# One weight load cut into other row groups: 96 + 8 + three strided groups of 8 rows in place of 112 + 5 + 5 + 5 + 1

## The chip, the cores and the metric

The kernel runs on one core of one Trainium2 chip. The metric is device time in microseconds (us) of the whole program on that core, the median of several runs. A profiled execution gives, beside its own time, a span (first to last instruction on the core) and a trace of instructions, semaphore events and DMA packets. Sixteen DMA engines move all data between HBM (the chip's main memory) and SBUF (the core's working memory).

## The reference, cut to what matters

Two stages follow each other. Attention over 4 batches, 8 heads, 768 positions and 64 head dimensions comes first; its output, reshaped to 3072 x 512, feeds a soft mixture of 8 experts. The weights of the experts are `w1` (8 x 512 x 1024) and `w2` (8 x 1024 x 512), in float32: 16 matrices of 2 MB each, 33.5 MB in all.

```python
logits = x @ phi
d = softmax(logits, axis=0);  slot_input = d.T @ x          # 32 slots, 4 of each expert
for e in range(E):
    slot_out[e] = maximum(slot_input[e] @ w1[e], 0) @ w2[e]
c = softmax(logits, axis=1);  out = c @ slot_out            # 3072 x 512
```

All the weights are read whole, however few the rows that go through them (4 slots for each expert).

## The kernel before, in words

One function builds the whole program. It describes the work as operations with dependences, costs and keys (`pl.op`), and a planner (`Plan.run`, L87) puts them into one order ahead of time; the order in which each engine gets its instructions follows from that. The planner's costs decide nothing at run time beyond the order.

**Loads.** q, k, v and the weights are loaded by the helper `dma` (L281). It makes three planner operations: the issue (a `gpsimd.dma_start`, so the instruction stands in POOL's queue, L283), the generation of the descriptors, and the landing (`dma_us`, L290, a cost by bytes and descriptors). The transfer converts float32 to bfloat16 on its way. There are 37 such transfers in one fixed order (the list `names`, L901, in which `w5` stands for five). All run on one software queue, called q0 in the profile, and each is spread over the DMA engines, which take their shares of the queue in the same order. An issue is planned behind the landing of the transfer eight places ahead of it (L907).

**A weight matrix as rows.** A `w1` matrix is seen as 128 rows (`(di do) f -> di do f`, `do=4`): row `di` is 16 KB of contiguous float32 in HBM and goes to SBUF partition `di`, where it takes 8 KB as bfloat16. A matrix loaded in one transfer of 128 rows (L364) gives each of 16 engines 8 rows.

**The uneven weight.** Matrix number `UNEVEN = 5` (`w5`, the sixth of `w1`) is the exception: the block at L355 to L363 loads it in five transfers into the one slot, and `landed w5` gathers them. The order of the queue around it is w3, w4, the five parts of w5, the rest of q and all of k and v of the last batch (`q3.64`, `k3.0`, `v3.0`), then w6 to w15. The last matrix, w15, comes in two halves of its columns (`w15a`, `w15b`, L350), 128 x 8 pieces each.

**The end of the program.** When attention is done, the matmuls of `w1` (L945) and then those of `w2`, expert by expert (`W2.0` to `W2.8`, emitted at L990), wait for the weights as they land. `W2.7` uses w15a and `W2.8` uses w15b. After each of the two, ACT scales the result (L1004), and PE, ACT and DVE form the output tiles (L1056, L1064, L1066). SP stores them on the hardware queue q1 (L1083): first six stores of 256 KB and one of 512 KB, then four of 1 MB.

Other traffic uses the same 16 engines: small tables and a first piece of w0 through q1 at the start, and fetches of instructions (queues q8 and q14), which the program does not issue itself.

Of the kernel before, what the change touches and what calls it, by code (L numbers as in the profile page):

```python
# [173 lines left out]
def kernel(  # L174
# [106 lines left out]
    def dma(name, key, nbytes, ndesc, buf, dst, src, deps=()):  # L281
        iss = pl.op("issue " + name, {"POOL": 0.62}, key, deps=deps, acq=[buf] if buf else [], lead=1.3,
                    emit=lambda o: nc.gpsimd.dma_start(dst(), src))  # L283
        issues.append(iss)
        gen = pl.op("gen " + name, {"GEN": 2.5 if name[0] == "w" and int(name[1:3].rstrip("abc")) > 5 else 1.45}, key, deps=[iss])
        land = pl.op("land " + name, {"DMA": dma_us(nbytes, ndesc) + LATE.get(name, 0.0)}, key, deps=[gen], lead=3.3)
        ring.setdefault(name, []).append((iss, land))
        return land

    def dma_us(nbytes, ndesc):  # L290
        return ndesc / 16 * 0.004 + nbytes / 16 / RATE
# [40 lines left out]
    def w_view(i):  # L332
        m = late_mem[i]() if i in late_mem else slots[wbuf[i].slot][:, :]
        return m.rearrange("p (a f) -> p a f", a=4 if i < NE else 8)

    def load_w(i, key, deps=()):
        if i == 0:

            flat = lambda: w_view(0).rearrange("p a f -> p (a f)")
            wland[0] = dma("w0", key, 7 << 18, 128, wbuf[0], lambda: flat()[:, WF:],  # L340
                           moe_w1[0].rearrange("(di do) f -> di (do f)", do=4)[:, WF:])
            w_cast.append(pl.op("CW", {"ACT": 0.6}, -90, deps=[wf_land], need=[wbuf[0]],
                                emit=lambda o: nc.scalar.copy(flat()[:, 0:WF], wf)))
            return
        if i < NE:
            src = moe_w1[i].rearrange("(di do) f -> di do f", do=4)
        else:
            src = moe_w2[i - NE].rearrange("(fi fo) d -> fi fo d", fo=8)
            if i == NW - 1:
                for k, (c0, c1) in enumerate(((0, CH), (CH, 512))):  # L350
                    last_lands.append(dma(f"w15{'ab'[k]}", key + 0.1 * k, (c1 - c0) << 12, 1024, None,
                                          lambda c0=c0, c1=c1: w_view(i)[:, :, c0:c1], src[:, :, c0:c1], deps=deps))
                wland[i] = last_lands[0]
                return
        if i == UNEVEN:  # L355

            buf, prev, land = wbuf[i], [], []
            for p0, p1 in ((0, 112), (112, 117), (117, 122), (122, 127), (127, 128)):
                land.append(dma(f"w{i}", key, (p1 - p0) << 14, p1 - p0, None if prev else buf,
                                lambda p0=p0, p1=p1: w_view(i)[p0:p1], src[p0:p1], deps=prev))  # L360
                prev = [issues[-1]]
            wland[i] = pl.op(f"landed w{i}", {"SP": 0.01}, key, deps=land)
            return  # L363
        wland[i] = dma(f"w{i}", key, 2 << 20, 128, None if i in late_mem else wbuf[i],  # L364
                       lambda: w_view(i), src, deps=deps)
# [151 lines left out]


    load_w(0, -30)
    for x in "ABC":  # L520
        load_tile(x, -29)
    load_w(1, -28)
    load_w(2, -27)
    for x in "DE":
        load_tile(x, -26)
# [103 lines left out]
    def evs(x, b, n):  # L629
        if b == 0:  # L630
            return ev[x, b]
        return [e for r0, r1, e in ev[x, b] if r0 < 24 * (n + 1) and r1 > 24 * n]
# [33 lines left out]
    for b in range(B):  # L666
        for n in range(4):
# [30 lines left out]
            for kk, g in enumerate(GORDER):  # L698
                sc = Buf("SC")
                key = k0 + kk * T / 5.3  # L700
# [17 lines left out]
                if g in (1, 3, 4):  # L718
                    m = {1: 0, 3: 1, 4: 2}[g]
                    masko[p, m] = pl.op(f"MK.{p}.{m}", {"DVE": [0.70, 0.70, 0.57][m]}, key + 0.3,  # L720
                                        deps=[expo[p, x] for x in ((0, 1), (2, 3), (3, 4))[m]] + o_hm[n],
                                        emit=mask_emit(b, n, m))

        for ns in ([(0, 1), (2, 3)] if b == 0 else [(0, 1, 2, 3)]):
            sc = Buf("SC")

            def emit_lx(o, b=b, sc=sc, ns=ns):
                sc_mms(sc, b, [(128 * x, n, XJ, XI, 1) for x, n in enumerate(ns)])

            key = T * (4 * b + ns[0]) + 0.9 * T  # L730
            a = pl.op(f"QX.{b}.{ns[0]}", {"PE": 0.09 * len(ns)}, key - 2.0, n=2 * len(ns),
                      deps=list(dict.fromkeys(e for n in ns for x in "qk" for e in evs(x, b, n))),
# [15 lines left out]
    for b in range(B):  # L748
        for n in range(4):
# [5 lines left out]
            for i in iorder:  # L755
                deps, need = [v2e[p], vfo[p]], set()
# [6 lines left out]
                def emit_pv(o, b=b, n=n, p=p, i=i):  # L763
                    pT = pTs[PTb[b, n].slot]
                    vb = vbs[VBb[b].slot]
                    for h in range(2):
                        for j in range(i + 1):
# [3 lines left out]
                            else:  # L771
# [5 lines left out]
                             deps=list(dict.fromkeys(deps)) + ([last] if last else []),  # L777
# [269 lines left out]
    for m, (gi, r, d0, d1) in enumerate(parts):  # L1047
# [7 lines left out]
        def emit_om(o, gi=gi, r=r, d0=d0, d1=d1, bank=bank, early=early):  # L1055
# [3 lines left out]
                  deps=[so_a if early else so_b], acq=[bf], emit=emit_om)  # L1059
# [8 lines left out]
        w = (d1 - d0) / 512  # L1068
# [39 lines left out]
    for o in order:  # L1108
# [9 lines left out]
        if front:  # L1118
# [3 lines left out]
            n = int(0.75 * (gap - 0.1) / unit + 0.5) if gap > 0.2 else 0  # L1122
# [23 lines left out]
        us, w = gap - (1.5 if o.name[:2] == "W2" else 0.12), 512 - c0  # L1146
# [53 lines left out]
```

## Time and profile before

| what | value |
|---|---|
| runs shown | 148.67, 148.75, 149.09 us; median 148.75 |
| profiled execution | 148.61 us, of which the span 146.8 (1.8 lie around it) |
| granted TensorE clock over the span | 0.965 |
| busy share of PE, DVE, ACT, POOL | 85%, 76%, 75%, 16% |
| q0 (software queue): packets, MB written | 6912, 26.09 |
| HBM read, written | 52.49 MB, 6.29 MB |
| w15b lands (last load) | 128.78 us into the span |
| last store of 1 MB lands | 145.9 us |

Times are in us from the start of the span, unless ns is written. A busy share is an average over stages that have different limits, so the views used below are the 40 slices of the span, the chain of work that ended last, the timeline around the last loads, and the DMA packets.

The trace holds two things of the DMA that are used below. For every transfer it has the 16 increments of its semaphore, one by each engine as its share has landed. For every packet it has the queue, the start, the duration and the size written, but not the engine. An engine runs its packets one behind the other, so that the packets can be joined into 16 chains by their starts; a chain is one engine, without its number.

### The profile page before, as it was taken

What the parts mean: (1) busy time and instruction counts of PE and PEld (TensorE: products, weight loads), DVE (VectorE), ACT (ScalarE), POOL (GpSimd) and SP (SyncE); (2) the same over time, 40 slices, a digit from 0 to 9 for tenths busy, and PEclk for the clock granted to TensorE, in tenths of its full rate; (3) what the DMA queues carried; (4) which work ended last, traced back from release to release, by engine and by line L of the source; (5) the groups of instructions that cost most, each with busy time, mean ns of one, the idle gap of its engine ahead of it and who ended that gap; (6) DMA issues with size and microseconds to landing.
All of it is one profiled execution on the core that took longest, in us unless ns stands there. A gap on an engine that the chain in (4) does not pass through costs nothing.

```text
span 146.8 us, 4972 instructions
## 1 busy us (share of the span) xinstructions
PE 125.4 (85%) x2171; PEld 80.9 (55%) x2171; DVE 111.6 (76%) x244; ACT 110.3 (75%) x143; POOL 24.0 (16%) x48
## 2 busy tenths in 40 slices
PE   6999899989899998999999999998778996679200
PEld 2365566668576675877576776765534564233000
DVE  3898399987999899899999999999847610249500
ACT  3374999989999999999998999999814700469600
POOL 6921110412011211110400211010700000100000
PEclk9999999999999999999999999999999999968955
DMA  4999999999999999999999999999999999979996
GB/s 100 190 214 215 225 204 211 218 210 228 214 206 212 215 223 214 219 214 203 211 216 224 212 214 219 216 216 214 214 219 214 216 215 186 137 246 392 413 415 250
DMA packets 9608, 33.03 MB, mean 225 GB/s; under 512 B 867, under 2 KB 4595, under 8 KB 7283
## 3 DMA queue, kind: packets, MB, share of 16 engines
q0 software_dynamic: 6912, 26.09, 88.8%
q1 hardware_dynamic: 2672, 6.62, 11.8%
q8 instruction: 17, 0.28, 0.7%
q14 instruction: 5, 0.04, 0.1%
q10 hardware_dynamic: 2, 0.00, 0.0%
HBM read 52.49 MB, written 6.29 MB: 400 GB/s over the span
## 4 chain that ended last, share of the span: by engine, by line
DMA 33%; PE 23%; DVE 15%; ACT 14%; POOL 4%; issue 4%; ACTq 0%; POOLq 0%
DMA slot<-in_v_dram 17%; DMA qk<-in_moe_w_dram 16%; ACT pt L713 9%; PE pv L773 7%; PE sc L641 6%; DVE pt L658 4%; DVE xv L787 3%; POOL slot L283 3%; PE tr L611 3%; DVE qk L278 2%; ACT slot L1064 2%; PE tr L799 2%; DVE xT L278 2%; PE tr L676 2%; PE sc L1056 1%
## 5 line engine op out<-in xcount | busy, mean ns | idle before, releaser
L713 ACT ACTIVATE pt<-sc 128x1024 bf16<-128x1024 f32 x80 | 76.8, 1045 | 3.0 <-PE sc L641 2.5
L641 PE MATMUL sc<-qk 64*128 64x512 bf16 (+3 forms) x256 | 31.2, 308 | 2.7 <-ACT pt L713 1.8
L658 DVE TENSOR_TENSOR pt<-pt,msk 128x1024 bf16<-128x1024 bf16 (+1 forms) x48 | 30.0, 640 | 0.5 <-ACT pt L713 0.4
L773 PEld LDWEIGHTS <-pt 128*128 128x128 bf16 x640 | 23.4, 97 | 6.7 <-issue 5.6
L773 PE MATMUL pv<-vx,pt 128*128 128x65 bf16 x352 | 26.1, 193 | 0.1
L773 PE MATMUL pv<-vf,pt 128*128 128x65 bf16 x288 | 20.9, 194 | 0.0
L641 PEld LDWEIGHTS <-qk 64*128 64x128 bf16 x256 | 10.3, 93 | 11.5 <-issue 4.5
L611 PE MATMUL tr<-ident,slot 128*64 128x128 bf16 (+1 forms) x448 | 15.5, 219 | 0.5 <-DMA slot<-in_v_dram 0.5
L787 DVE TENSOR_TENSOR xv<-pv,rs 128x768 bf16<-128x768 f32 x16 | 15.3, 957 | 0.6
L611 PEld LDWEIGHTS <-slot 128*64 128x64 bf16 (+1 forms) x448 | 12.7, 110 | 3.6 <-issue 3.2
L283 POOL DMA_DIRECT2D slot<-in_moe_w_dram x15 | 8.1, 541 | 39.8 <-PE tr L611 9.1
L278 DVE COPY qk<-tr 128x768 bf16<-128x768 bf16 (+2 forms) x24 | 12.9, 551 | 0.7 <-PE tr L611 0.4
L278 DVE COPY xv<-tr 128x768 bf16<-128x768 bf16 (+2 forms) x20 | 8.4, 432 | 2.9 <-PE tr L569 2.9
L799 PE MATMUL tr<-ident,xv 128*128 128x128 bf16 x96 | 8.1, 220 | 2.2 <-DVE xv L787 1.9
L278 DVE COPY xT<-tr 128x768 bf16<-128x768 bf16 x14 | 7.8, 554 | 1.0 <-PE tr L799 0.8
L1004 ACT ACTIVATE msk<-pv,rcs 128x256 bf16<-128x256 f32 x2 | 0.9, 474 | 10.0 <-PE pv L990 10.0
L799 PEld LDWEIGHTS <-xv 128*128 128x128 bf16 x96 | 5.7, 97 | 4.7 <-DVE xv L787 2.2
L1066 DVE TENSOR_SCALAR slot<-tr,rrow 128x256 f32<-128x256 f32 (+1 forms) x6 | 3.3, 571 | 6.5 <-PE tr L1056 6.4
L676 PE MATMUL tr<-ident,xv 128*128 128x128 bf16 x96 | 7.9, 220 | 0.1
L278 DVE COPY vx<-tr 128x768 bf16<-128x768 bf16 x14 | 7.7, 550 | 0.2 <-PE tr L676 0.2
L1157 PE MATMUL pv<-zero 128*128 128x512 bf16 x30 | 7.5, 382 | 0.0
L692 DVE TENSOR_TENSOR vf<-vx,fm 128x528 bf16<-128x528 bf16 x16 | 6.9, 430 | 0.3
(122 smaller groups left out, 172.3 us busy)
## 6 DMA issues: line engine op xcount, KB each, us to landing
slot<-in_moe_w_dram POOLq DMA_DIRECT2D x9, 1024.0 KB, 22.8
out_dram<-slot SPq DMA_DIRECT2D x4, 1024.0 KB, 5.9
slot<-in_q_dram POOLq DMA_DIRECT2D x3, 768.0 KB, 20.0
slot<-in_k_dram POOLq DMA_DIRECT2D x3, 768.0 KB, 15.1
slot<-in_moe_w_dram POOLq DMA_DIRECT2D x2, 896.0 KB, 23.1
slot<-in_v_dram POOLq DMA_DIRECT2D x2, 768.0 KB, 13.2
out_dram<-slot SPq DMA_DIRECT2D x6, 256.0 KB, 2.5
slot<-in_v_dram POOLq DMA_DIRECT2D x2, 512.0 KB, 24.2
```

The source lines that it names most:

```text
L278: nc.vector.tensor_copy(dst, src)
L283: emit=lambda o: nc.gpsimd.dma_start(dst(), src))
L611: nc.tensor.transpose(t[64 * i:64 * (i + 1), :, s, :], rv[:, i, 8 * c + s, :], ident[0:nr, 0:nr])
L641: nc.tensor.matmul(scb[sc.slot][:, i, c:c + 128 * nb], kk, qq.rearrange("p b c -> p (b c)"), start=True, stop=True)
L658: nc.vector.tensor_tensor(pw, pw, mw, op=ALU.mult)
L676: nc.tensor.transpose(t[:, 128 * j:128 * (j + 1)], vT[:, 6 * n + j, :], ident)
L692: nc.vector.tensor_tensor(vfs[VFb[p].slot], vv, fm[:, n], op=ALU.mult)
L713: nc.scalar.activation(pTs[PTb[b, n].slot][:, :, 512 * g:512 * (g + 1)], scb[sc.slot], ACT.Exp, scale=scale)
L773: nc.tensor.matmul(pvb[:, h, 65 * i:65 * (i + 1)], lt, rhs, start=(j == 0), stop=(j == i))
L787: nc.vector.tensor_tensor(xo, pvw[:, :, :, 0:64], r.rearrange("p i (j o) -> p i j o", o=1).to_broadcast([P, 2, 6, 64]), op=ALU.mult)
L799: nc.tensor.transpose(t[:, 128 * i:128 * (i + 1)], xv[:, i, 128 * n:128 * (n + 1)], ident)
L1157: nc.tensor.matmul(bank[:, c0:c0 + w], zero[:, 0:128], zero[:, 0:w], start=(c0 == 0), stop=True, skip_group_check=True)
```

## The change

The five transfers of `w5` take other rows. All five still go into the same slot, in the same place of the same queue, and every row is still loaded once. A third number, the step, is added to the row ranges, so that the last three transfers take every third row from 104 on: rows 104, 107, ... 125, then 105, ... 126, then 106, ... 127.

```diff
         if i == UNEVEN:
 
             buf, prev, land = wbuf[i], [], []
-            for p0, p1 in ((0, 112), (112, 117), (117, 122), (122, 127), (127, 128)):
-                land.append(dma(f"w{i}", key, (p1 - p0) << 14, p1 - p0, None if prev else buf,
-                                lambda p0=p0, p1=p1: w_view(i)[p0:p1], src[p0:p1], deps=prev))
+            for p0, p1, st in ((0, 96, 1), (96, 104, 1), (104, 128, 3), (105, 128, 3), (106, 128, 3)):
+                n = len(range(p0, p1, st))
+                land.append(dma(f"w{i}", key, n << 14, n, None if prev else buf,
+                                lambda p0=p0, p1=p1, st=st: w_view(i)[p0:p1:st], src[p0:p1:st], deps=prev))
                 prev = [issues[-1]]
             wland[i] = pl.op(f"landed w{i}", {"SP": 0.01}, key, deps=land)
             return
```

The row counts were 112, 5, 5, 5, 1 and become 96, 8, 8, 8, 8. The change's own title says that three rows more go to eight DMA engines, where they went to five.

## The prediction

> **What bounds the kernel now.** I read the 40 slices first, then the chain of work that ended last, then the timeline around the last loads, then the DMA packets.
>
> ```profile
> DMA  4999999999999999999999999999999999979996
> GB/s 100 190 214 215 225 204 211 218 210 228 214 206 212 215 223 214 219 214 203 211 216 224 212 214 219 216 216 214 214 219 214 216 215 186 137 246 392 413 415 250
> ```
>
> The DMA engines are full from the second slice to the 34th, at one rate. The dip in slices 34 and 35 (121 to 128.4 us) is the end of the loads; after it come the stores.
>
> ```profile
> 103.77 0.53 POOL pt L283
> 104.30 0.28 POOL qk L283
> 104.58 0.60 issue
> 105.17 23.61 DMA qk<-in_moe_w_dram
> 128.78 0.04 issue
> 128.82 0.43 PE pv L990 x8
> 129.25 0.02 issue
> 129.27 0.48 ACT msk L1004
> 129.75 0.04 issue
> 129.79 0.32 PE sc L1056
> ```
>
> In the chain, w15b is issued at 104.6 and lands 23.6 us later: it stands in a full queue. From 128.78 on everything hangs on it. The timeline shows that PE was ready:
>
> ```profile
> 128.08 0.27 PE L1056 MATMUL tr<-msk,expT 128*128 128x256 bf16 x1
> ...
> 128.28 0.09 PEld L990 LDWEIGHTS <-xT 128*32 128x32 bf16 x1 [0.22 <-issue]
> 128.82 0.40 PE L990 MATMUL pv<-qk,xT 128*32 128x256 bf16 x8 [0.47 <-DMA qk<-in_moe_w_dram]
> ```
>
> PE had the stationary matrix in at 128.28 + 0.09 and waited 0.47 us for the DMA. So the kernel is bound by the engine whose share of w15b lands last; from there to the end of the span it is 146.8 - 128.78 = 18.0 us. What was done ahead of it hangs on w15a, which the same engine brings last.
>
> **Sixteen engines, not one queue.** The 16 increments of three transfers, sorted, in us (from the trace's semaphore events):
>
> ```
> w4    63.51 63.61 63.66 63.85 63.89 64.00 64.01 64.38 | 64.72 64.73 64.77 64.80 64.83 64.91 64.92 65.12
> w6    81.42 81.48 81.80 | 82.53 82.61 82.62 82.72 82.94 83.13 83.49 83.55 83.66 83.67 83.85 83.99 84.53
> w15b  125.67 125.72 126.05 | 127.67 127.73 127.77 127.87 127.90 127.92 127.97 127.98 128.09 128.09 128.30 128.36 128.78
> ```
>
> Ahead of w5 eight engines lead by about 1 us; at the end three lead by about 2 us, and thirteen lie within 1.2. The packets say why. A row of a weight (8 KB written) comes every 606 ns on each engine. Queue q8 fetches 16 KB of instructions 16 times up to 117 us; such a packet takes 0.89 to 0.98 us and holds its engine up. Followed as chains, each of the eight late engines gets one of the eight fetches after w4; together with their lag at w4 that makes two each (an inference for the earlier ones). The three that lead keep exactly the same distances from 76 us to the end: no fetch at all. I call the eight late ones F (fetch) and the others N.
>
> Now w5 itself. After its 112-row transfer five chains, all in N, each show a row, an increment, a row, an increment, a row, an increment: the three transfers of 5 rows went to the same five engines, one row each. They take 6.20 us from the end of w4 to the end of w5, the rest of N 4.36: 1.84 us for three rows, about what two fetches cost. The single row 127 was cut into 16 pieces of 512 bytes, 41 ns each beyond their overlap. So the five are level with F at the end, and three engines of N have 2 us to spare.
>
> The last engine of all (128.78) is one of the five. At 80.04 a fetch of 8 KB on q14 falls into its chain, and its next row takes 838 ns instead of 625: 0.53 us in all. The last of F lands at 128.36.
>
> **The change part by part.**
>
> *Even part, 6 rows in place of 7.* 96 rows over 16 engines are 6 each. Each engine loses a row: -606 ns.
>
> *Rows 96 to 103.* The title's three rows more, for eight engines, fit only if these eight rows are shared evenly, half a row each (6.5 against 9.5). The trace has no such transfer. Its neighbours are the contiguous single row, cut into 16 pieces, and the contiguous 5 rows, not cut. Half a row is a packet of 4 KB, which other loads show: 304 ns from start to start. Bounds: half a row on each engine; a whole row on N and nothing on F; nothing on N and a whole row on F. I take the half row, since 8 rows, unlike 5, make 16 equal pieces of at most a row, as the title needs.
>
> *The strided rows.* Three transfers of 8 rows in place of three of 5. By the nearest row, 5 rows on the same five engines three times, I put them one each on the same eight engines, the five and the three others of N. A row costs 604 ns and its increment 21, as before: 1.88 us for three. An engine without a row passes such a transfer in 11 ns. A step in HBM and SBUF leaves the row at 16 KB read, 8 KB written; nothing shows another price. If a strided row cost more, the five have 0.34 us before they are later than now.
>
> *The row that falls away.* Row 127 alone: -41 ns, with its increment kept by the fifth transfer.
>
> The sums from the end of w4 to the end of w5, from these rows:
>
> - F: 4.26 + 0.03 + 0.06 = 4.36 before; 6 rows 3.655 + half row 0.325 + empty transfers 0.034 = 4.01 after: **-0.34**.
> - The five: 6.20 before; 3.655 + 0.325 + 1.878 = 5.86 after: **-0.34**.
> - The other three: 4.36 before, 5.86 after: **+1.50**. They land at 126.05 + 1.50 = 127.55 at the latest.
>
> The largest landing goes from 128.78 to 128.44, still by the same engine, while F ends at 128.02. The bytes are the same: thirteen engines give up 0.34 each (4.4 us together), which three that had idled take over (3 x 1.50).
>
> *What doesn't move.* POOL issues five transfers for w5 as before, 0.50 to 0.58 us each, and the queue holds over 20 us of work (w15b: 24 us from issue to landing), so a slower issue is hidden; it would cost only if the queue ran dry. In the planner the bytes up to the fifth part are equal, so q3.64 and all that follows keep their planned landings; only the planned issues of w6 to w9 can move, and they stand in POOL's queue, which between 72 and 103 us holds little else. From 31 to 104 us the chain is compute, so an earlier landing there brings nothing; the three delayed engines are still not the last for k3.0 and v3.0. What is late next: the same transfer, then PE, whose first half also moves by 0.34 since w15a ends 2.65 us before w15b on every engine. The stores start from the results, so I move the 18.0 us behind as a block.
>
> So the profiled time of 148.61 becomes 148.27, and the median, 0.14 above it, 148.75 - 0.34 = **148.41 us**, -0.23%. About 0.3% (0.45 us) is what a measurement of this kernel can tell from no change.
>
> **The rivals.**
>
> 1. *The first eight rows go whole to N too.* Then N gets 10 rows, F 6. The five: 3.655 + 4 x 0.626 = 6.16, -0.04; F -0.66; the three +1.80 (127.85). End 128.74: 148.71, no change. For it: the 5-row transfers were not cut. Against: the title's count of three. The Trainium skill, "DMA: Bandwidth & Descriptors", section "Why a DMA increments its semaphore by 16 and not by 1", has an exception for the software queue in which each engine gets the partitions divided by 16, rounded up, from engine 0 on; the trace's five engines agree, and eight rows would then go this way.
>
> 2. *The stride doesn't hold rows together, or the eight alternate.* All 16 engines then get 8 rows: F 3.655 + 4 x 0.325 = 4.96, +0.60, or with whole rows in turn +0.57. The five gain 1.2, but F now ends at 128.36 + 0.6 = 128.96: 148.93, slower by 0.12%. The decision is at F +0.42. Half a way (first eight rows cut, the three others in turn) gives F +0.28: 128.64, 148.6. For it: the trace has no strided rows. Against: three transfers in a row hit the same five. The same section of the skill states that fewer than 16 engines are taken from a round-robin cursor, which speaks for this rival; the trace's chains of three rows speak against it here.
>
> 3. *Three of the eight engines are fetch engines*, ending clearly slower. The trace gives no numbers to engines; that the three next to the five are the three idle ones I infer from the five all lying in N. An F engine with 9.5 rows gets +1.50: 127.67 to 128.36 become 129.17 to 129.86. It decides as soon as one lands behind 128.78, as every F engine would. Of three the last at about 129.6: +0.85, 149.6 us.
>
> 4. *First eight rows whole on F, the rest on N* (7 against 9): F -0.04, the five -0.66, end 128.32: 148.29. This is the largest gain that F allows.
>
> **How the numbers follow.** Forecast 60%; rival 1 14%; rival 2 11%; rival 3 9%; rival 4 3%; 3% for a step that I don't see (a reordered queue, another granted clock in the last stage, 0.72 now). Forecast with run spread (148.67 to 149.09 for one kernel) 148.2 to 148.65. The range, 148.15 to 149.0, takes in rivals 1, 2 and 4 and leaves out rival 3. Faster by over 0.3% means below 148.30: a quarter of the forecast's cases, half of rival 4's and a little of the rest: 0.22. Slower, above 149.20: rival 3, a little of rival 2 and of the unseen: 0.14. Within: 0.64.
>
> **What would show it right or wrong.** After: eight chains with three whole rows behind the increment of the first part, 16 packets of 4 KB in place of the 16 of 512 bytes, no engine that leads by 2 us in w15b, and its last landing near 128.44. Three leaders still there, or a new last one above 129, mean rival 3; 32 whole rows behind the first part mean rival 1; a spread of F to the back by half a microsecond, rival 2. It is wrong in its last step if w15b lands earlier and the end doesn't follow.

## The result, and the profile after

The changed kernel takes 149.79 us (median of 5 runs, 149.56 to 150.19) beside 148.74 for the kernel before (5 runs, 148.55 to 149.09): ratio 1.0074, 95% interval 1.0050 to 1.0099. That is slower by 1.05 us, where 0.34 less was forecast, and outside the range.

The 40 slices of the page of the changed kernel (profiled execution 149.56 us, span 147.8):

```profile
DMA  4999999999999999999999999999999999779995
GB/s 97 193 213 218 218 209 211 212 214 220 217 212 217 211 223 217 220 215 199 208 216 224 215 217 211 217 213 215 215 217 217 220 204 186 102 240 382 410 426 248
```

Up to the 34th slice the DMA digits are those of the kernel before. The 35th, at the end of the loads, has fallen from 9 to 7 tenths (137 to 102 GB/s); the 36th was at 7 already. The views by stage put numbers to it. Each line has the stretch, its length, the busy time of PE, PEld, DVE, ACT and POOL, and at its end the granted clock, the DMA share and GB/s. The kernel before:

```profile
125.60:128.80 3.20, 1.52 (x15) 0.88 (x15) 1.26 (x3) 1.78 (x4) 0.40 (x1) 1.00 0.81 114
128.80:146.80 18.00, 7.43 (x32) 2.91 (x31) 6.89 (x12) 7.91 (x14) 0.00 (x0) 0.72 0.90 350
```

The changed kernel:

```profile
126.70:129.90 3.20, 1.52 (x19) 0.89 (x18) 1.27 (x3) 1.78 (x4) 0.40 (x1) 1.00 0.44 63
129.90:147.80 17.90, 7.38 (x32) 2.81 (x31) 6.91 (x12) 7.90 (x14) 0.00 (x0) 0.73 0.90 352
```

In the last 3.2 us of the loads the DMA engines are 44% busy, where they were 81%: many have finished, and the loads wait for a few. The stage behind, 17.9 us, is as long as it was, within 0.1 us. The chain that ended last:

```profile
103.67 0.53 POOL pt L283
104.20 0.28 POOL qk L283
104.48 0.60 issue
105.07 24.77 DMA qk<-in_moe_w_dram
129.85 0.04 issue
129.89 0.43 PE pv L991 x8
```

w15b is issued 0.1 us earlier than before and lands at 129.85, 1.07 later. PE stood ready again, as the timeline has it:

```profile
129.36 0.09 PEld L991 LDWEIGHTS <-xT 128*32 128x32 bf16 x1 [0.22 <-issue]
129.89 0.40 PE L991 MATMUL pv<-qk,xT 128*32 128x256 bf16 x8 [0.46 <-DMA qk<-in_moe_w_dram]
```

The wait for the DMA is 0.46 us, where it was 0.47: what comes ahead of it has moved along with w15a. So the loss is that one landing: it moved by 1.07 us, and the span is 1.0 us longer. Its 16 increments, before and after:

```
before  125.67 125.72 126.05 | 127.67 127.73 127.77 127.87 127.90 127.92 127.97 127.98 128.09 128.09 128.30 128.36 128.78
after   125.08 125.35 | 127.33 127.43 127.46 127.46 127.57 127.70 127.70 127.71 128.00 128.08 128.23 128.64 | 129.68 129.85
```

Two engines still lead by 2 us, and two others are now a microsecond behind the rest. The DMA issues name the five parts of w5:

```profile
slot<-in_moe_w_dram POOLq DMA_DIRECT2D x1, 768.0 KB, 29.5
slot<-in_moe_w_dram POOLq DMA_DIRECT2D x4, 64.0 KB, 21.2
```

Four parts of 64 KB written, 8 whole rows each. The packets show how they were shared. There is no packet of 4 KB more than before, and of 512 bytes exactly 16 fewer (2048 on q0): rows 96 to 103 were not halved. The chains from the end of w4 on (left: end of w4 in ns; R a packet of 8 KB, | an increment, ' the 9 ns records of a transfer that brings nothing to this engine, h a 4 KB packet of q3.64):

```
N  63225 RRRRRR|R|R|R|R|hhhh|
N  63538 RRRRRR|R|R|R|R|hhhh|
N  63769 RRRRRR|R|R|R|R|hhhh|
F  64376 RRRRRR|R|R|R|R|hhhh|
F  64392 RRRRRR|'''''''hhhh|
```

Eight chains have four rows behind the sixth, the other eight none: 10 rows against 6. And the eight are not N: six of N and two of F (64376 and 64562). The two have the latest landings. By the terms of the prediction an engine with 10 rows takes 3.655 + 4 x 0.626 = 6.16 us for w5, where F took 4.36: +1.80, and the latest of F, 128.36, would be 130.16 at most, the earliest 129.47. The two are at 129.68 and 129.85.

### The profile page after: what moved, and what is told of

Read it like the earlier page. It is cut to its first block, busy times and chain, and to the rows that moved or that the text cites. A ratio compares the mean times of both kernels' runs of the same rounds, so it can differ in the third digit from the quotient of the medians.

```text
span 147.8 us, 4972 instructions
## 1 busy us (share of the span) xinstructions
PE 124.7 (84%) x2171; PEld 80.6 (55%) x2171; DVE 111.8 (76%) x244; ACT 110.2 (75%) x143; POOL 23.9 (16%) x48
## 4 chain that ended last, share of the span: by engine, by line
PE 28%; DMA 24%; ACT 20%; DVE 16%; issue 4%; POOL 1%; ACTq 1%; POOLq 0%
DMA qk<-in_moe_w_dram 17%; ACT pt L714 14%; PE sc L642 7%; DMA slot<-in_k_dram 7%; PE pv L774 7%; DVE pt L659 4%; PE tr L612 4%; DVE xv L788 3%; DVE qk L278 2%; ACT slot L1065 2%; PE tr L570 2%; DVE xT L278 2%; PE tr L677 1%; PE tr L800 1%; DVE xv L278 1%
```

## The experiments

**Theory A (place).** A software-queue transfer of fewer than 16 whole rows puts one row on each of the first n places of a fixed order, always from the same start, whatever the step. The first eight places are six engines of N and two of F. **Rival B:** the step led rows elsewhere, or the strided rows cost more. **Rival C:** transfers start at another engine each time. **Rival D:** the loss grows with the number of rows moved, not with single engines.

All edits are to the block of the uneven weight. Where only the line with the row ranges is shown, the lines below it are those of the changed kernel.

**The eight without a step.**

```diff
-            for p0, p1, st in ((0, 96, 1), (96, 104, 1), (104, 128, 3), (105, 128, 3), (106, 128, 3)):
+            for p0, p1, st in ((0, 96, 1), (96, 104, 1), (104, 112, 1), (112, 120, 1), (120, 128, 1)):
```

> The changed kernel, with its three strided groups taken as contiguous rows (96 + 8 + 8 + 8 + 8). Theory A (place): a transfer of fewer than 16 rows puts one whole row on each of the same first engines of a fixed order, whatever the step; the eight are six engines without fetches and two with. Then nothing changes against the changed kernel: eight chains with four rows, two of them fetch engines, w15b lands last near 129.8, about 149.8 us, 0.7% over the kernel before. Rival B (step): the step is what led rows to other engines; contiguous rows go to the eight without fetches, two leaders vanish, w15b lands near 128.7, 148.7 us, as before.

Measured: 149.56 us beside 148.37 for the kernel before on that chip; ratio 1.0074 (1.0052 to 1.0097), the changed kernel's own. The chain:

```profile
104.78 25.09 DMA qk<-in_moe_w_dram
129.87 0.04 issue
```

The last landing is 129.87, and two leaders (125.47, 125.70) and two laggards (129.49, 129.87) are there again. The step of 3 makes no difference here. B falls for the changed kernel.

**The five with a step.**

```diff
-            for p0, p1 in ((0, 112), (112, 117), (117, 122), (122, 127), (127, 128)):
+            for p0, p1, st in ((0, 112, 1), (112, 127, 3), (113, 127, 3), (114, 127, 3), (127, 128, 1)):
```

> The kernel before, with its three groups of 5 rows taken with a step of 3 (rows 112, 115, ... 124 and so on). Theory A: the same five engines, three rows each, 606 to 626 ns a row; no change from the kernel before (148.7, within 0.3%). Rival B (step): the rows go to other engines or cost more; chains with other counts, or over 650 ns a row, and w15b lands 0.3 to 1.5 us later: 149.0 to 150.2.

Measured: 148.64 beside 148.37, ratio 1.0012 (0.9997 to 1.0027). The chain:

```profile
105.03 23.71 DMA qk<-in_moe_w_dram
128.74 0.04 issue
```

w15b lands at 128.74 (before: 128.78), with three leaders at 125.44 to 125.81. Five chains, all in N, have three rows each behind the 112. So a row taken with a step of 3 has no price that these runs show, and no other place.

**Ladders.** Transfers of falling size turn a place into a count: an engine at place 4 takes part in all that have more than 4 rows.

```diff
+            for p0, p1, st in ((0, 80, 1), (80, 93, 1), (93, 101, 1), (101, 108, 1), (108, 114, 1), (114, 119, 1), (119, 123, 1), (123, 126, 1), (126, 128, 1)):
```

> w5 in transfers of 80 (5 rows an engine), 13, 8, 7, 6, 5, 4, 3 and 2 contiguous rows, so that an engine's count behind its first five rows tells its place in the order. Theory A: counts 8, 8, 7, 6, 5, 4, 3, 2, then five of 1 and three of 0; the counts 5 to 8 all on engines without fetches, and of the counts 4, 3 and 2 one on such an engine and two on fetch engines. Rival C (rotating start): each transfer begins at another engine, so the counts lie close together (2 to 4) and don't follow this ladder. The time (13 rows on two engines, about 1.8 us over now) is no matter here.

The chains that can be read without doubt, five rows ahead of the first increment:

```
N  63267  8 rows more      N  64177  6      N  63380  2      F  64382  4
N  63605  8                N  63353  5      N  63463  1      F  64493  3
N  63302  7                N  63321  0      F  64749  0      F  64904  0
```

8, 8, 7, 6, 5 are all on N; 4 and 3 on F; 2 on N again. So the order begins with five engines of N, then two of F, then one of N. The time was 151.28 us in one run, with 13 rows on two engines.

```diff
+            for p0, p1, st in ((0, 80, 1), (80, 92, 1), (92, 103, 1), (103, 113, 1), (113, 122, 1), (122, 128, 1)):
```

> w5 as 80, 12, 11, 10, 9 and 6 contiguous rows: counts behind the first five rows are 5 on the first six places, 4 on the next three, then 3, 2, 1 and four of 0. It tells which of the ninth to thirteenth place is the one engine there without fetches that the first ladder left open. Theory A: exactly one of the counts 4, 4, 3, 2, 1, 0 of those places is on an engine without fetches, besides the eighth place (4) and one of the last three (0). No time is forecast.

On N the counts are five times 5, two of 4 and one 0; on F 5, 4, 2, 1 and several 0, with one chain not certain. The second 4 on N is place 8, since places 5 and 6 are F. So the seventh N engine is place 8 and the eighth among the last four (149.80 us in one run).

```diff
+            for p0, p1, st in ((0, 48, 1), (48, 63, 1), (63, 77, 1), (77, 90, 1), (90, 102, 1), (102, 113, 1), (113, 123, 1), (123, 128, 1)):
```

> w5 in transfers of 48 (3 rows an engine), 15, 14, 13, 12, 11, 10 and 5 contiguous rows: the ladder for the upper places. Theory A: counts 7 on five engines, 6 on five, then 5, 4, 3, 2, 1, 0; two of the last six or of the lower ones are engines without fetches, six are fetch engines. It tells whether the engines without fetches are one run of places that goes round the end (say the last two and the first six) or lie apart. Rival C (rotating start): no ladder.

This one is mostly a miss: with so many rows in step the chains cross at the same nanoseconds and few can be followed. One can: a chain of N (w4 at 63449) has its three rows and then none, which only place 15 has. One run, 150.88 us. Places 0 to 4, 7, 8 and 15 are then N, and 5, 6 and 9 to 14 F. That N lies in one piece with the five, which the prediction needed, is wrong.

**One place more than five.**

```diff
+            for p0, p1, st in ((0, 96, 1), (96, 110, 1), (110, 116, 1), (116, 122, 1), (122, 128, 1)):
```

> w5 as 96, 14, 6, 6 and 6 contiguous rows: the first six places get 10 rows each, the next eight 7, the last two 6. One place more than the five of the kernel before, where the changed kernel has three more. Theory A (place): the sixth place is a fetch engine; it alone gets 10 rows and ends as late as in the changed kernel, w15b at 129.7 to 129.9, so the whole loss is there at once: 149.4 to 149.8, 1.006 to 1.009 of the kernel before. Rival D (share): the loss grows with the number of rows moved; with 3 of the 9 moved rows it is a third, 1.002 to 1.003. If the sixth place were an engine without fetches: no loss, 1.000.

Measured: 149.80 beside 148.63, ratio 1.0075 (1.0050 to 1.0100). The chain:

```profile
104.84 24.81 DMA qk<-in_moe_w_dram
129.65 0.04 issue
129.69 0.43 PE pv L991 x8
```

One increment is at 129.65 and the next at 128.70: a single engine, the chain with w4 at 64348, in F, with four rows behind the sixth. D falls; a third of the move costs all of the loss. The price is one engine's, and the kernel pays the largest.

**9 against 7.**

```diff
+            for p0, p1, st in ((0, 112, 1), (112, 128, 2), (113, 128, 2)):
```

> w5 as 112 rows and two strided groups of 8: the first eight places get 9 rows, the others 7. Theory A: the two fetch engines among the eight have one row less than in the changed kernel, so they land 0.65 us earlier, at 129.05 to 129.2, 0.3 to 0.45 us behind the kernel before: 1.002 to 1.004. Rival B (step) or another cause that has nothing to do with the rows on two engines: the loss stays at 1.007.

Measured: 149.24 beside 148.63, ratio 1.0051 (1.0023 to 1.0080), above the 1.002 to 1.004 that was expected, though the interval holds most of that. The chain:

```profile
105.27 24.19 DMA qk<-in_moe_w_dram
129.46 0.04 issue
```

The two chains of F with two rows behind the seventh (w4 at 64291 and 64776) land at 128.94 and 129.46. The first is earlier than was expected, the second later, since its engine was later at w4 than the two of the changed kernel (64376 and 64562). From w4 on both take what the terms give: 4.261 + 1.252 for w5. The interval alone doesn't part this from the changed kernel's loss; the chains do.

**Rows in four runs.**

```diff
-            for p0, p1, st in ((0, 96, 1), (96, 104, 1), (104, 128, 3), (105, 128, 3), (106, 128, 3)):
-                n = len(range(p0, p1, st))
...
-                                lambda p0=p0, p1=p1, st=st: w_view(i)[p0:p1:st], src[p0:p1:st], deps=prev))
+            for p0, p1, c0, c1 in ((0, 112, 0, 1024), (112, 120, 0, 512), (112, 120, 512, 1024), (120, 128, 0, 512), (120, 128, 512, 1024)):
+                n = p1 - p0
...
+                                lambda p0=p0, p1=p1, c0=c0, c1=c1: w_view(i)[p0:p1, :, c0:c1], src[p0:p1, :, c0:c1], deps=prev))
```

> w5 as 112 rows and two groups of 8 rows, each in two halves of the columns, so that a row is four separate runs of 2 KB. It asks which rule of the Trainium skill, page DMA: Bandwidth and Descriptors, section Why a DMA increments its semaphore by 16 and not by 1, holds for a transfer that is not whole rows. Theory A (same first engines): eight chains get all four halves. Rival C (round-robin start): the halves alternate between the eight first and the eight last, two on each engine. With A the two fetch engines have 9 rows' bytes, about 1.003 of the kernel before; with C all have 8, about 1.001.

The 128 packets of 1 KB come in 32 groups of four, 8 groups in each of the four transfers. Eight groups start 21 ns behind an increment that ends a share with data: those are the first transfer's, behind the 112 rows. The other 24 start behind the 9 ns records of a transfer that brought that engine nothing. So no engine took part in two transfers in a row: they alternate, two for each engine. Here rival C holds: a transfer of 8 rows that are not contiguous takes the next eight engines. The one execution took 150.88 us, but an engine of it was late already ahead of w5 (w4 landed at 67.47, in the kernel before at 65.12), so its time says nothing.

## Why the prediction was wrong, point by point

**Right.** The bound (the last landing of w15b), the two groups of engines, the five engines of the 5-row transfers, the prices of a row (606, 626 with its increment) and the block behind: the landing moved by 1.07, the span by 1.0, the median by 1.05. Strided rows without a price and without an effect on the planner's order also hold: the kernel with strided fives is within its interval of the kernel before.

**Wrong, first: "Half a row on each engine."** The eight rows 96 to 103 went whole to the first eight places, as rival 1 had it. I took the title's count of three rows more as what decides between the bounds, but the difference is four rows (10 against 6); the nearest row, five whole rows on five engines, was the better guide. The term was -0.34 for F and came to -0.66 for six of its engines, +1.80 for two. Alone it would have cost the forecast its gain (rival 1: 128.74).

**Wrong, second, and decisive: "on the same eight engines, the five and the three others of N".** The next three places are F, F and N. The two of F got four rows more than the other six of F and landed w15b at 129.68 and 129.85, where 128.44 was forecast as the last landing. This is rival 3's mechanism, which had 9%, with two engines in place of three. Rival 3 priced an F engine at +1.50 (9.5 rows); with 10 rows it is +1.80. That its 149.6 us came so close to 149.79 is in part luck. What I had was five engines, all in N; that the group goes on in the same order was not in any row. The trace before has no engine numbers and no group of six to fifteen rows, so it couldn't say which engine is the next one. One engine more was enough: the run with six places shows the whole loss.

**Combined rivals.** I priced rivals 1 and 3 apart and gave neither much. Both happened, with the signs named for them (32 whole rows behind the first part; a new last landing above 129), and the range, which left out rival 3, didn't hold the time.

**Which of two rules.** The Trainium skill's exception for the software queue ("DMA: Bandwidth & Descriptors", section "Why a DMA increments its semaphore by 16 and not by 1"), by which some copies spread their partitions, divided by 16 and rounded up, over the engines from the first on, fits the transfers of whole rows that could be followed here, of 2 to 13 rows: the same places from the first on. That section's other rule, by which a transfer that uses fewer than 16 engines takes the next ones from a round-robin cursor, fits the rows in four runs. The trace tells which of the two applies here.

**Open.** Why the fetches go to places 5, 6 and 9 to 14 isn't shown; nor is it shown that the order of places is the engines' numbering. A version that gives more rows to places 7, 8 and 15 alone was not tried; by the order found here, a group of whole rows that reaches places 7 and 8 also reaches 5 and 6. Such a version could gain at most what evens out all engines: the mean of the increments before is 127.62, the last 128.78. Of the last one, 0.53 is the fetch on q14 in that engine's chain. In the changed kernel the like fetch (at 79.91; the next row takes 846 ns) falls, by the steps between the packets, into a chain of N with ten rows (w4 at 63889). That chain's share of w15b lands at 128.64, ahead of the two of F, so it doesn't set the end there.

## What to carry to other kernels

When a load is bound by its slowest DMA engine, price the change for each engine and take the largest; a mean or a sum over engines shows a gain where one engine loses. Ahead of moving rows to "the next" engines, run a ladder of transfers of falling size: one execution showed here which of the first eight places carry other traffic, and the later places took further runs. Here a transfer of few whole rows was steered by its row count, not by the step of 2 or 3 between the rows.

## What the runs showed of the hardware that was not expected

Between w4 and 117 us there are eight instruction fetches of 16 KB (0.89 to 1.28 us each). They go one each to the eight engines that are late at w4, and to none of the other eight, in the kernel before and in the changed kernel; that the eight ahead of w4 went to the same engines is inferred from that lag. These eight engines are places 5, 6 and 9 to 14. The others are free of the 16 KB fetches only: the 8 KB fetches of q14 at 80.04 and 107.76 in the kernel before fall into chains of N. Whole rows in groups of 2 to 13 always start at the same place, while 8 rows in four runs of 2 KB take turns between the two halves (one execution). A single row alone is cut into 16 pieces, but 5, 6 or 8 contiguous rows are not.
